# Batches and heads change places in an attention with routed experts: loads, stores, denominators and the order of the work

## The chip, the cores and the metric

One core of a Trainium2 chip runs the kernel. The metric is the device time of one execution in microseconds (us), the median of several runs.

## The reference

Two stages follow each other. First a linear attention over q, k, v of shape (8 batches, 8 heads, 576 tokens, 64), all float32:

```python
def phi(x):
    proj = np.einsum('bhsd,df->bhsf', x, w_phi)              # 64 -> 128 features
    proj = proj - np.max(np.abs(proj), axis=-1, keepdims=True)
    return np.concatenate([np.exp(proj), np.exp(-proj)], axis=-1)
q_p, k_p = (phi(q), phi(k))
kv = np.einsum('bhsf,bhsd->bhfd', k_p, v)
z = np.sum(k_p, axis=2)
num = np.einsum('bhsf,bhfd->bhsd', q_p, kv)
den = np.einsum('bhsf,bhf->bhs', q_p, z)[..., None] + 1e-06
attn = num / den
```

Its output is 4608 tokens of 512 values. Then 8 experts: `logits = x @ w_gate` are sorted over all tokens and experts at once, each token goes to the first expert in that order that still has room (576 tokens each), and each expert computes `relu(x @ w1) @ w2` with 512, 1024 and 512 columns.

## The kernel before, in words

**Units.** The attention goes by 16 units; a unit is a pair of batches and a pair of heads. Of the 128 rows of every tile, one half belongs to one member of a pair and the other half to the other. In a unit the steps are, by the names used below:

- SyncE issues the loads: ki and qi (`loadx`, L131, through `raw`, L116: 8 DMAs of 72 KB each, in pieces of 32 rows) and vi (`loadv`, L125: two DMAs of 64 rows). ki, qi and vi have two buffers each.
- VectorE transposes blocks (kt, qt, L183: kT and qT).
- TensorE projects k and q in three groups each (kg, qg, L194; 72 matmuls of 64x64, 24 a group), VectorE takes the largest magnitude (kgm, qgm, L198) and subtracts it (kgs, qgs, L201); for two of the k groups ScalarE copies (kgc, L207) and GpSimd subtracts (L210).
- ScalarE takes the exponentials of k (ke, L222: kP), TensorE multiplies with v (kv, L241, three groups of 24), GpSimd sums kP over the tokens (ad, L231 and L232: ks).
- ScalarE copies kv (kvT, L245), TensorE multiplies it with the gate weights beside an identity (bd, L257), ScalarE copies the result (kz, L260), TensorE sums ks over the rows (z, L272, the denominators, 32 matmuls of 64x64 against ones), VectorE puts that beside kz (zk, L274).
- TensorE transposes the q part (T, L288), ScalarE takes its exponentials (ex, L292: qP), TensorE multiplies (num, L305, 144 matmuls of 128x64, in two groups), and VectorE divides (x0 and x1, L309 to L320: xp). A store takes xp to memory (xs): ScalarE issues it for the first 13 units, SyncE for the last three (L325). GpSimd adds the logits (lg, L331 to L333).

A matmul on float32 stands as two instructions in the trace, so the counts here are of the trace's instructions.

**What sets the order.** Class `Plan` keeps a list of steps, each with an engine, a duration, a due time and what it waits for. In the attention `strict` is on: on each engine the steps stand in the order of their due times, 16 a unit apart plus an offset out of the table `ATT['o']` (`place`, L152; rows '0', '1', 's' for all units between, '9' for the last). Every engine's queue is in order, so a step that waits holds what stands behind it. In addition each k load from unit 4 on waits for the first exponentials of the unit two before it (L135 and `kel`). Seven matmuls on zeros (L111) keep TensorE busy before the first data.

**After the attention** comes the routing (a search by digits of the logits, small steps of VectorE and TensorE), and then the experts, whose order `Plan` works out from the due times in the table `MOE` and modelled durations. Their products are h (L885) and y (L915, L930).

Of the kernel before, what the change touches and what calls it, by code (L numbers as in the profile page):

```python
# [17 lines left out]
class Plan:  # L18
# [3 lines left out]
    SEM=40.; strict=False; dl=0.; wp=6.; fetch=0.; at=16.; edge=193.; ready=0.  # L22
# [5 lines left out]
    def order(self):  # L28
# [7 lines left out]
        while left:  # L36
# [61 lines left out]
def attention(ctx, tc, nc, q, k, v, w_phi, w_gate, xs, L, C, xp, cfg={}, after=None, later=None, count=None, init=iter(())):  # L98
# [3 lines left out]
    d=dict(TI=17.,ldk=60.,ldq=50.,ldv=45.,kt=-8.,kg=0.,ks=3.,kv=8.,kvs=1.,bd=1.,z=5.,qt=-4.,qg=4.,qs=3.,T=5.,num=20.,ns=4.,stay=3.,init=-6.,nqP=4,pools=(('kg',0),('kg',1)),nkt=3,nqt=3,ad=4.,st=5.,sem=85.,pr=6.,prs=2.5,fetch=3700.)  # L102
# [8 lines left out]
    for _ in range(cfg.get('nwarm',7)): PE.matmul(p[:,0],w[:,0:128],w,start=True,stop=True)  # L111
# [4 lines left out]
    def raw(eng,t,x,u,bi):  # L116

        bp,hp=divmod(u,NP)
        for a in range(2):
            for db in range(2):  # L120
                o=bass.AP(tensor=x.tensor,offset=x.offset+((2*bp+bi)*H+2*hp+a)*HS+32*db,ap=[[18*D,32],[D,18],[1,32]])
                i=eng.dma_start(t[64*a+32*db:64*a+32*db+32,bi],o)  # L122
                if a==db==0: first=i
        return first
# [6 lines left out]
    def loadx(nm,x,u):  # L131
        t=T[nm,u]=sb.tile([128,2,18,32],F32,name=nm+'i',bufs=2)
        for bi in range(2):
            i=raw(nc.sync,t,x,u,bi)
            if nm=='k' and u>3 and bi==(u>7): tc.add_manual_dep(i.ins,T['kel',u-2].ins.name,mybir.DependencyInfo(mybir.DependencyClass.Sync,mybir.DependencyReason.DATA),reason='behind the exponentials')  # L135

    T['k',0]=sb.tile([128,2,18,32],F32,name='ki',bufs=2); T['q',0]=sb.tile([128,2,18,32],F32,name='qi',bufs=2)
    raw(nc.sync,T['k',0],k,0,0); raw(nc.scalar,T['k',0],k,0,1)
    raw(nc.sync,T['q',0],q,0,0); raw(nc.scalar,T['q',0],q,0,1)
    P=Plan(d['stay']*1e3); P.SEM=d['sem']; P.fetch=d['fetch']  # L140
    P.add(('boot',-1),'SP',8900.,-1e3,lambda x: None)
    P.add(('aboot',-1),'ACT',10300.,-1e3,lambda x: None)
# [9 lines left out]
    def place(name,eng,u,due):  # L152

        t=d.get('o')
        if t is None: return due
        if name=='st' and eng=='ACT': return u*16.+66.7
        if eng=='X': return due
        if name=='ldv' and eng=='SP': return u*16.+t['1'].get('ldv.SP',t['s']['ldq.SP']+.01)
        return u*16.+t['s' if eng=='SP' else {0:'0',1:'1',NU-1:'9'}.get(u,'s')][(name if isinstance(name,str) else ''.join(map(str,name)))+'.'+eng]
    def unit(u):  # L160
# [8 lines left out]
        if not first:  # L169
            add('ldk','SP',6600.,-d['ldk'],lambda x: loadx('k',k,u),slot=slots(('ki',2)),lat=4000.)  # L170
            add('ldq','SP',6600.,-d['ldq'],lambda x: loadx('q',q,u),slot=slots(('qi',2)),lat=4000.)
            if u>1: add('ldv','SP',1300.,-d['ldv'],lambda x: loadv(u),slot=slots(('vi',2)),lat=5000.)
            else: add('ldv','X',0.,-d['ldv'],lambda x: loadv(u,G),slot=slots(('vi',2)),after=9000.)
        else:
            add('ldv','X',0.,-d['ldk'],lambda x: loadv(u,G),slot=slots(('vi',2)),after=9000.)
            for nm in 'kq': add('ld'+nm,'X',0.,-d['ldk'],lambda x: None,slot=slots((nm+'i',2)))

        def blocks(nm,aft):

            for bi in range(2):  # L180
                def f(x,bi=bi):
                    if bi==0: T[nm+'T',u]=sb.tile([128,2,9,32,2],F32,name=nm+'T',bufs=2)
                    V.transpose(T[nm+'T',u][:,bi].rearrange('p s t l -> p l s t'),T[nm,u][:,bi])  # L183
                add((nm+'t',bi),'DVE',662.,d[nm+'t']+.7*bi,f,['ld'+nm],slot=slots((nm+'T',2)) if bi==0 else (),frees=((nm+'i',u),),after=aft[u][bi] if u<len(aft) else 0.,seq=(nm+'t',0) if bi else None)
        def project(nm,g,s0,s1,due,src):
# [16 lines left out]
            add((nm,g),'PE',n*(218. if not first else 480. if nm=='kg' else 340.),due,pe,[(src[0]+'t',0),(src[0]+'t',1)],'Q',slots(('g',NG,nm,g)),((src,u),),ins=16*n+.5)  # L202
# [45 lines left out]
        def bd(x):  # L248
            p=T['bdp',u]=pair(('g',u,'bd'))(x)
            t=T['kvT',u]  # L250
            for i in range(2):
                for fh in range(2):
                    for a in range(2):
                        r=slice(64*a,64*a+64)
                        for c in range(2):
                            o=128*fh+64*c
                            PE.matmul(p[64*c:64*c+64,a,72*(2*i+fh):72*(2*i+fh)+72],t[r,i,o:o+64],C['bd'][r,hp,:],start=True,stop=True)  # L257
# [5 lines left out]
        def z(x):  # L263
            p=T['zp',u]=pair(('g',u,'z'))(x)
            ks=T['ks',u]
            for a in range(2):
                for fh in range(2):
                    for i in range(2):
                        r=slice(64*i,64*i+64)
                        for c in range(2):  # L270
                            o=128*fh+64*c
                            PE.matmul(p[64*c:64*c+64,i,2*(2*fh+a):2*(2*fh+a)+2],ks[r,a,o:o+64],C['one'][r,0:2],start=True,stop=True)  # L272
        def zk(x):
            V.tensor_copy(T['kz',u].rearrange('p i h a e -> p i (h a) e')[:,:,:,72],T['zp',u][:,:,0:8:2])  # L274
        add('z','PE',430.,kend+d['z'],z,[('ad',8)],'Q',slots(('g',NG,'z')),(('ks',u),),ins=65)
        add('zk','DVE',180.,kend+d['z']+.5,zk,['z','kz'],frees=(('g',u,'z'),))

        blocks('q',((12600.,12700.),))
        for g,(s0,s1) in enumerate(SG):
# [13 lines left out]
            add(('T',g),'PE',2*n*62.,due+d['T'],tr,[('qgs',g)],'P',slots(('g',NG,'T',g)),(('qgt',u,g),),ins=8*n+1)  # L293
# [71 lines left out]
def consts(ctx,tc,nc,w_phi):  # L365
# [7 lines left out]
    nc.vector.tensor_scalar(ident,jp,0.0,None,op0=OP.is_equal)  # L373
    one=cp.tile([128,128],F32,name='one'); nc.vector.memset(one,1.0); C['one']=one
    return C

def weights(ctx,tc,nc,w_gate,C):
    cp=ctx.enter_context(tc.tile_pool(name='wts',bufs=1))
    W=dict(C)
    bd=cp.tile([128,4,72],F32,name='bd'); W['bd']=bd  # L380
    g=w_gate.rearrange('(h a d) e -> a d h e',a=2,d=64)
    for i in range(2):
        r=slice(64*i,64*i+64)
        nc.vector.tensor_copy(bd[r,:,8-8*i:72-8*i],C['ident'][r,None,64*i:64*i+64].to_broadcast([64,4,64]))
        nc.gpsimd.dma_start(bd[r,:,64*i:64*i+8],g[i])
# [568 lines left out]
MOE = {'TE': 48.88, 'ch': -31.55, 'cp': 1.18, 'w1': 52.42, 'w2': 22.65, 'xt': 37.52, 'hl': -10.26, 'g': -10.06, 'y': 48.5, 'w20': 11.59, 'c1': -22.58, 'cp1': 0.52, 'stay': 7.96, 'sem': 96.08, 'wp': 124.82}  # L954
# [58 lines left out]
```

## Time and profile before

| | us |
|---|---|
| three runs | 776.07, 777.0, 781.02 (median 777.0) |
| the profiled execution | 778.89 |
| its span, first to last instruction | 777.1 |
| busy: PE | 735.8 (95%) |
| PEld (weight loads) | 640.2 (82%) |
| DVE (VectorE) | 563.0 (72%) |
| ACT (ScalarE) | 348.2 (45%) |
| POOL (GpSimd) | 310.0 (40%) |

PE is TensorE, SP is SyncE; SPq and ACTq are the queues in which they issue transfers. A row of a timeline has its start, its length, the engine, the line, what is written and read, and in brackets how long the engine stood idle before it and what ended that. The granted clock (PEclk) is a share of full speed.

### The profile page before, as it was taken

How to read it: one execution, taken by the hardware profiler on the slowest of the kernel's cores; microseconds unless marked ns; L12 is line 12 of the kernel's file. 1: busy time of each engine (PE TensorE's matmuls, PEld its weight loads, DVE VectorE, ACT ScalarE, POOL GpSimd, SP SyncE). 2: the span in 40 equal slices, each digit the busy share in tenths (PEclk: the TensorE clock that was granted, in tenths of full speed). 3: DMA queues.
4: the chain of work that ended last, by engine and by line, in shares of the span. 5: the costliest groups of instructions: out<-in, count | busy, mean ns of one | idle time of the engine just before them, and what ended most of it. 6: DMA issues, size and time to landing. Idle time of an engine off the chain costs nothing.

```text
span 777.1 us, 25979 instructions
## 1 busy us (share of the span) xinstructions
PE 735.8 (95%) x11090; PEld 640.2 (82%) x11090; DVE 563.0 (72%) x1489; ACT 348.2 (45%) x609; POOL 310.0 (40%) x331
## 2 busy tenths in 40 slices
PE   5988999899999995899999999999999999999997
PEld 3777888888888885598798898898897897897995
DVE  7985988788889867898597597696696795671410
ACT  2775776677766650343243333333332422352411
POOL 6877788688778750201302202203104104301102
PEclk9998999999999995899999999999999999999999
DMA  9677878777776211534505505505406407601301
GB/s 152 98 141 146 161 137 168 146 153 148 141 138 141 68 35 32 169 110 139 191 11 154 183 5 163 177 2 181 158 2 196 143 1 237 244 29 42 129 14 47
DMA packets 206403, 91.95 MB, mean 118 GB/s; under 512 B 154784, under 2 KB 189632, under 8 KB 206288
## 3 DMA queue, kind: packets, MB, share of 16 engines
q1 hardware_dynamic: 179952, 61.89, 33.8%
q0 software_dynamic: 6416, 20.15, 7.8%
q10 hardware_dynamic: 19920, 8.26, 3.9%
q8 instruction: 87, 1.43, 0.7%
q14 instruction: 28, 0.23, 0.1%
HBM read 71.39 MB, written 18.87 MB: 116 GB/s over the span
## 4 chain that ended last, share of the span: by engine, by line
PE 73%; issue 13%; DVE 4%; DMA 3%; ACT 2%; POOL 2%; SPq 2%; POOLq 0%; ACTq 0%; DVEq 0%
PE h L885 20%; PE y L915 17%; PE g L305 10%; PE g L241 7%; PE g L194 6%; PE y L930 3%; PE g L288 3%; SPq L122 2%; DMA qi<-in_q_dram 2%; DMA ki<-in_k_dram 2%; PE rps L619 1%; PE g L257 1%; PE rps L615 1%; PE h L853 1%; POOL out_dram L945 1%
## 5 line engine op out<-in xcount | busy, mean ns | idle before, releaser
L945 POOL DMA_INDIRECT out_dram<-ysb,idx x40 | 42.4, 1059 | 331.0 <-ACT ysb L938 328.4
L232 POOL TENSOR_TENSOR ks<-ks,kP 128x512 f32<-128x512 f32 x112 | 143.0, 1277 | 21.9 <-ACT kP L222 15.6
L885 PE MATMUL h<-xh,w1h 128*128 128x272 f32 (+3 forms) x512 | 141.6, 301 | 0.0
L885 PE MATMUL h<-xh,w1l 128*128 128x272 f32 (+3 forms) x512 | 140.5, 296 | 0.2 <-DVE w1l L826 0.2
L897 ACT ACTIVATE fh<-h 128x272 fp32r<-128x272 f32 (+2 forms) x128 | 49.2, 386 | 128.9 <-PE h L885 103.9
L915 PE MATMUL y<-w2h,fh 128*128 128x512 f32 x256 | 101.8, 398 | 0.0
L915 PE MATMUL y<-w2h,fl 128*128 128x512 f32 x256 | 100.8, 394 | 0.0
L915 PE MATMUL y<-w2l,fh 128*128 128x512 f32 x256 | 100.7, 394 | 0.0
L885 PEld LDWEIGHTS h<-xh,w1l 128*128 128x128 f32 x512 | 96.7, 189 | 0.4 <-DVE w1l L826 0.4
L885 PEld LDWEIGHTS h<-xh,w1h 128*128 128x128 f32 x512 | 96.1, 189 | 1.0 <-ACT xh L858 0.5
L885 PE MATMUL h<-xl,w1h 128*128 128x272 f32 (+3 forms) x512 | 92.6, 298 | 0.0
L305 PE MATMUL g<-kz,qP 128*64 128x73 f32 x2304 | 85.6, 235 | 5.8 <-issue 5.5
L305 PEld LDWEIGHTS g<-kz,qP 128*64 128x64 f32 x2304 | 81.4, 143 | 8.8 <-issue 7.4
L292 ACT ACTIVATE qP<-g 128x768 f32<-128x768 f32 x96 | 70.8, 811 | 19.3 <-PE g L288 16.8
L222 ACT ACTIVATE kP<-kgt 128x768 f32<-128x768 f32 x96 | 74.0, 837 | 10.9 <-DVE kgt L201 6.7
L901 DVE SCALAR_TENSOR_TENSOR fl<-h,fh 128x272 fp32r<-128x272 f32 (+2 forms) x128 | 52.8, 417 | 32.9 <-ACT fh L897 18.2
L938 ACT COPY ysb<-y 128x512 f32<-128x512 f32 (+1 forms) x40 | 21.8, 546 | 121.9 <-issue 79.6
L885 PEld LDWEIGHTS h<-xl,w1h 128*128 128x128 f32 x512 | 75.7, 188 | 0.1
L241 PE MATMUL g<-kP,vi 64*64 64x256 f32 x1152 | 73.8, 377 | 1.8 <-ACT kP L222 1.7
L860 DVE TENSOR_TENSOR xl<-h,xh 128x512 fp32r<-128x512 f32 (+1 forms) x40 | 24.3, 626 | 56.1 <-ACT xh L858 54.8
L241 PEld LDWEIGHTS g<-kP,vi 64*64 64x64 f32 x1152 | 46.5, 133 | 13.2 <-ACT kP L222 2.2
L915 PEld LDWEIGHTS y<-w2l,fh 128*128 128x128 f32 x256 | 48.2, 188 | 9.9 <-issue 0.2
(203 smaller groups left out, 1334.9 us busy)
## 6 DMA issues: line engine op xcount, KB each, us to landing
raww<-in_moe_w_dram SPq DMA_DIRECT2D x64, 512.0 KB
ki<-in_k_dram SPq DMA_DIRECT2D x124, 72.0 KB
qi<-in_q_dram SPq DMA_DIRECT2D x124, 72.0 KB
vi<-in_v_dram SPq DMA_DIRECT2D x28, 288.0 KB
xs<-xp ACTq DMA_DIRECT2D x13, 576.0 KB
xs<-xp SPq DMA_DIRECT2D x3, 576.0 KB
vi<-in_v_dram POOLq DMA_DIRECT2D x4, 288.0 KB
xg<-xs,idx POOLq DMA_INDIRECT x40
```

The source lines that it names most:

```text
L194: PE.matmul(p[64*bi:64*bi+64,a,128*(s-s0):128*(s-s0)+128],t[r,bi,s,:],C['w'][r,:],start=True,stop=True)
L222: for i in range(2): z=A.activation(o[:,:,:,128*i:128*i+128],t,AF.Exp,scale=1.0-2*i)
L232: else: G.tensor_add(ks,ks,kP[:,s])
L241: PE.matmul(p[64*a:64*a+64,i,0:256],v_[r,a,s,:],kP[r,s,a,:],start=s==0,stop=s==8,skip_group_check=True)
L292: for fh in range(2): A.activation(t[:,fh].rearrange('p i a s t -> p i (a s t)'),p,AF.Exp,scale=1.0-2*fh)
L305: PE.matmul(p[64*ab:64*ab+64,a,73*(j-j0):73*(j-j0)+73],T['qP',u,j//3][:,fh,ab,a,j%3,:],T['kz',u][:,ab,fh,a,:],start=fh==0,stop=fh==1)
L860: p,h,l=T['xv',r,b0,i]; V.tensor_sub(l,p,h)
L885: PE.matmul(p,ws[:,k,o:o+128],xx[:,k,o1:o2],start=n==0,stop=n==11)
L897: A.activation(hh[:,f,o1:o1+m1],p[:,0:m1],AF.Relu)
L901: V.scalar_tensor_tensor(hl[:,f,o1:o1+m1],p[:,0:m1],0.0,hh[:,f,o1:o1+m1],op0=OP.max,op1=OP.subtract)
L915: PE.matmul(p,hx[:,f,o:o+128],ws[:,f%2,:],start=n==0,stop=n==23)
L945: st=G.indirect_dma_start(out=ov,out_offset=bass.IndirectOffsetOnAxis(ap=iv,axis=0),in_=yv,in_offset=None)
```

## The change

Of a unit's four batch and head combinations, the row halves now hold the two heads of one batch and the free dimension the two batches; before it was the other way round. Two heads lie next to each other in memory, so v comes with one DMA of 128 rows. The denominators take both row halves at once, against a matrix `sel` with ones in one half per column, 16 instructions of 128x64 in place of 32 of 64x64. All stores are issued by SyncE. The waits of k loads for exponentials are gone. 33 warm-up matmuls stand in place of 7; kt and qt tiles have 4 buffers in place of 3, qP 5 in place of 4. The tables of due times are new, with rows of their own for units 2 ('2') and 14 ('8') too, and the `MOE` table has new values.

```diff
-    for _ in range(cfg.get('nwarm',7)): PE.matmul(p[:,0],w[:,0:128],w,start=True,stop=True)
+    for _ in range(cfg.get('nwarm',33)): PE.matmul(p[:,0],w[:,0:128],w,start=True,stop=True)
...
-                o=bass.AP(tensor=x.tensor,offset=x.offset+((2*bp+bi)*H+2*hp+a)*HS+32*db,ap=[[18*D,32],[D,18],[1,32]])
+                o=bass.AP(tensor=x.tensor,offset=x.offset+((2*bp+a)*H+2*hp+i)*HS+32*db,ap=[[18*D,32],[D,18],[1,32]])
...
-        for i in range(2):
-            o=bass.AP(tensor=v.tensor,offset=v.offset+((2*bp+i)*H+2*hp)*HS,ap=[[9*D,64],[HS,2],[1,9*D]])
-            eng.dma_start(t[64*i:64*i+64].rearrange('p h s d -> p h (s d)'),o)
+        o=bass.AP(tensor=v.tensor,offset=v.offset+(2*bp*H+2*hp)*HS,ap=[[9*D,128],[H*HS,2],[1,9*D]])
+        eng.dma_start(t.rearrange('p h s d -> p h (s d)'),o)
...
-            if nm=='k' and u>3 and bi==(u>7): tc.add_manual_dep(i.ins,T['kel',u-2].ins.name,mybir.DependencyInfo(mybir.DependencyClass.Sync,mybir.DependencyReason.DATA),reason='behind the exponentials')
...
-                    for i in range(2):
-                        r=slice(64*i,64*i+64)
-                        for c in range(2):
-                            o=128*fh+64*c
-                            PE.matmul(p[64*c:64*c+64,i,2*(2*fh+a):2*(2*fh+a)+2],ks[r,a,o:o+64],C['one'][r,0:2],start=True,stop=True)
+                    for c in range(2):
+                        o=128*fh+64*c; e=2*(2*fh+a)
+                        PE.matmul(p[64*c:64*c+64,0,e:e+2],ks[:,a,o:o+64],C['sel'],start=True,stop=True)
...
-                                PE.matmul(p[64*ab:64*ab+64,a,73*(j-j0):73*(j-j0)+73],T['qP',u,j//3][:,fh,ab,a,j%3,:],T['kz',u][:,ab,fh,a,:],start=fh==0,stop=fh==1)
+                                PE.matmul(p[64*ab:64*ab+64,a,73*(j-j0):73*(j-j0)+73],T['qP',u,j//3][:,fh,a,ab,j%3,:],T['kz',u][:,a,fh,ab,:],start=fh==0,stop=fh==1)
...
-            (A if out_ else nc.sync).dma_start(o,T['x',u][:,:,8:136])
-        out_=u<13
-        add('st','ACT' if out_ else 'SP',700.,d['num']+d['ns']+d['st'],st,[('x',1)],lat=3500.,frees=(('xb',u),))
+            nc.sync.dma_start(o,T['x',u][:,:,8:136])
+        add('st','SP',d['sp'],d['num']+d['ns']+d['st'],st,[('x',1)],lat=3500.,frees=(('xb',u),))
...
-    for u in range(4,NU): P.by[('ldk',u)]['deps'].append((('ke',0),u-2))
```

What the new due times say, sorted by engine, for a unit u in the steady part:

| engine | before | after |
|---|---|---|
| SyncE | k(u), v(u-1), q(u) | st(u-4), q(u), v(u-1), k(u) |
| TensorE | kg0, kg1, kv0(u-1), kg2, qg2, kv1(u-1), qg0, kv2(u-1), qg1, bd(u-1), z(u-1), T2, T0, num0(u-1), num1(u-1), T1 | kg0, kv0(u-1), kg1, kg2, kv1(u-1), qg0, kv2(u-1), qg2, bd(u-1), qg1, z(u-1), T0, T2, num0(u-1), num1(u-1), T1 |
| ScalarE | the store of u-2 behind the first exponentials of u | no store |

On VectorE, x1(u-2) stands just ahead of the maxima of kg0(u), with the second q transpose of unit u right behind those. In SyncE's new order the k load of unit 14 stands between those of units 7 and 8, and VectorE's two transposes of it stand in units 7 and 9.

## Rows read from the trace of the kernel before

**Rows 1.** Busy time in stretches: length, engines busy (instructions), PEclk, DMA share, GB/s

```profile
60.00:80.00 20.00, 16.92 (x436) 15.58 (x432) 12.11 (x19) 10.74 (x15) 13.02 (x11) 0.83 0.80 161
440.13:497.13 57.00, 57.00 (x456) 49.39 (x457) 43.42 (x148) 19.91 (x43) 10.70 (x15) 1.00 0.36 117
```

**Rows 2.** Timeline of TensorE, undisturbed units and the last one: start, length

```profile
78.33 1.54 PE L194 MATMUL g<-w,kT 64*64 64x128 f32 x48
...
88.45 4.79 PE L305 MATMUL g<-kz,qP 128*64 128x73 f32 x144
...
93.69 1.54 PE L194 MATMUL g<-w,kT 64*64 64x128 f32 x48
...
261.38 1.54 PE L194 MATMUL g<-w,kT 64*64 64x128 f32 x48
...
283.65 6.40 PE L305 MATMUL g<-kz,qP 128*64 128x73 f32 x144
```

**Rows 3.** Timeline of TensorE, 56 to 78 us

```profile
56.17 0.89 PE L194 MATMUL g<-w,kT 64*64 64x128 f32 x24 [1.45 <-ACT qP L292]
...
68.05 0.77 PE L257 MATMUL g<-bd,kvT 64*64 64x72 f32 x32 [3.08 <-ACT kvT L245]
...
70.98 6.90 PE L305 MATMUL g<-kz,qP 128*64 128x73 f32 x144
```

**Rows 4.** Timeline of ScalarE and its queue, 51 to 68 us

```profile
51.05 0.58 ACTq L325 DMA_DIRECT2D xs<-xp  x1
51.68 3.05 ACT L222 ACTIVATE kP<-kgt 128x768 f32<-128x768 f32 x4 [2.65 <-DMA qi<-in_q_dram]
...
66.81 0.56 ACTq L325 DMA_DIRECT2D xs<-xp  x1
67.41 0.58 ACT L245 COPY kvT<-g 128x512 f32<-128x512 f32 x1 [4.28 <-DMA qi<-in_q_dram]
```

**Rows 5.** Busy time in stretches around one stop of TensorE

```profile
134.00:137.00 3.00, 2.97 (x108) 2.63 (x106) 2.97 (x6) 2.15 (x5) 2.04 (x2) 1.00 1.03 256
137.00:140.00 3.00, 1.00 (x30) 1.00 (x32) 1.22 (x2) 2.91 (x5) 2.65 (x3) 1.00 0.61 93
140.00:143.00 3.00, 3.00 (x60) 3.00 (x58) 0.84 (x3) 1.51 (x2) 2.84 (x3) 0.55 0.93 205
```

**Rows 6.** Waits: total us, times, longest (TensorE 78-262, SyncE 60-250, VectorE 0-300)

```profile
PE g L305 <- issue: 5.3, 6, 2.0
PE g L288 <- issue: 0.9, 1, 0.9
...
SPq L122 <- ACT kP L222: 10.6, 8, 2.6
...
DVE rd L309 <- PE g L305: 30.4, 26, 3.8
```

**Rows 7.** Queues of the page: packets, MB, share of 16 DMA engines

```profile
q8 instruction: 87, 1.43, 0.7%
```

**Rows 8.** Timeline of SyncE's queue, one unit's loads

```profile
180.15 7.31 SPq L122 DMA_DIRECT2D ki<-in_k_dram  x8
187.56 2.19 SPq L130 DMA_DIRECT2D vi<-in_v_dram  x2
189.86 6.57 SPq L122 DMA_DIRECT2D qi<-in_q_dram  x8
```

**Rows 9.** Timeline of TensorE, bd and the denominators of one unit

```profile
86.43 0.73 PE L257 MATMUL g<-bd,kvT 64*64 64x72 f32 x32
86.98 0.59 PE L272 MATMUL g<-one,ks 64*64 64x2 f32 x32
```

**Rows 10.** Timeline of TensorE, warm-up, first projection, later matmuls on zeros

```profile
1.36 3.17 PE L111 MATMUL g<-warm 128*128 128x512 bf16 x7 [1.36 <-DVE warm L109]
10.22 4.32 PE L194 MATMUL g<-w,kT 64*64 64x128 f32 x72 [5.70 <-DVE kT L183]
...
319.88 1.03 PE L582 MATMUL y<-onesb 128*128 128x512 bf16 x4
```

More of the change, by code (lines that the diff above doesn't have):

```diff
@@ L18 @@
 class Plan:
-    SEM=40.; strict=False; dl=0.; wp=6.; fetch=0.; at=16.; edge=193.; ready=0.
+    SEM=40.; strict=False; dl=0.; wp=6.; fetch=0.; at=16.; edge=193.; ready=0.; sw=(45.,45.)
     def __init__(self,stay=0.): self.t=[]; self.by={}; self.stay=stay
@@ L77, in order @@
             if e=='PE':
-                if mode[0] not in (None,x['mode']): s+=95.
-                if mode[0]!=x['mode'] or s>free.get(e,0.)+1.: s+=100. if x['mode']=='A' else 50.
+                if mode[0] not in (None,x['mode']): s+=45.
+                if mode[0]!=x['mode'] or s>free.get(e,0.)+1.: s+=self.sw[x['mode']!='A']
                 mode[0]=x['mode']
@@ L183, in f @@
                     V.transpose(T[nm+'T',u][:,bi].rearrange('p s t l -> p l s t'),T[nm,u][:,bi])
-                add((nm+'t',bi),'DVE',662.,d[nm+'t']+.7*bi,f,['ld'+nm],slot=slots((nm+'T',2)) if bi==0 else (),frees=((nm+'i',u),),after=aft[u][bi] if u<len(aft) else 0.,seq=(nm+'t',0) if bi else None)
+                add((nm+'t',bi),'DVE',662.,d[nm+'t']+.7*bi,f,['ld'+nm],slot=slots((nm+'T',2)) if bi==0 else (),frees=((nm+'i',u),),after=aft if first else 0.,seq=(nm+'t',0) if bi else None)
         def project(nm,g,s0,s1,due,src):
@@ L201, in sub @@
                 V.tensor_sub(t,vw(),T[nm+'m',u,g].to_broadcast([128,2,n,128]))
-            add((nm,g),'PE',n*(218. if not first else 480. if nm=='kg' else 340.),due,pe,[(src[0]+'t',0),(src[0]+'t',1)],'Q',slots(('g',NG,nm,g)),((src,u),),ins=16*n+.5)
+            add((nm,g),'PE',n*(218. if not first else d['cold'][nm]),due,pe,[(src[0]+'t',0),(src[0]+'t',1)],'Q',slots(('g',NG,nm,g)),((src,u),),ins=16*n+.5)
             add((nm+'m',g),'DVE',dv(256*n),due+.8,mx,[(nm,g)])
@@ L256, in bd @@
                             o=128*fh+64*c
-                            PE.matmul(p[64*c:64*c+64,a,72*(2*i+fh):72*(2*i+fh)+72],t[r,i,o:o+64],C['bd'][r,hp,:],start=True,stop=True)
+                            PE.matmul(p[64*c:64*c+64,a,72*(2*i+fh):72*(2*i+fh)+72],t[r,i,o:o+64],C['bd'][r,272*hp+72*i:272*hp+72*i+72],start=True,stop=True)
         def kz(x):
@@ L354, in some @@
                 if i<NI-1: break
-        P.add(('init',i),'DVE',270. if i<7 else 200.,-100.+i if i<7 else 457.+.001*i,some,[('init',i-1)] if i else [],lat=95.,after=3900.)
+        early=i<d['ni']
+        P.add(('init',i),'DVE',300. if early else 200.,(-100.+i if d.get('o') is None else d['o']['i']['init%d'%i]) if early else 457.+.001*i,some,[('init',i-1)] if i else [],lat=95.,after=d['iaft'])
+        if not early: P.t[-1]['key']=('F','late')
+    P.by[(('pr',0),NU-NP-1)]['deps'].append(('init',d['ni']-1))
     P.strict='o' in d
-    for u in range(4,NU): P.by[('ldk',u)]['deps'].append((('ke',0),u-2))
     out=P.order()
@@ L373, in consts @@
     nc.vector.tensor_scalar(ident,jp,0.0,None,op0=OP.is_equal)
+    sel=cp.tile([128,2],F32,name='sel'); C['sel']=sel
+    nc.vector.memset(sel,0.0)
+    for i in range(2): nc.vector.memset(sel[64*i:64*i+64,i:i+1],1.0)
     one=cp.tile([128,128],F32,name='one'); nc.vector.memset(one,1.0); C['one']=one
@@ L379, in weights @@
     W=dict(C)
[L380 to L385, printed above, removed]
+    bd=cp.tile([128,4*272],F32,name='bd'); W['bd']=bd
+    g=w_gate.rearrange('(h d) e -> d h e',d=64)
+    for a in range(2):
+        r=slice(64*a,64*a+64)
+        nc.vector.tensor_copy(bd.rearrange('p (h z) -> p h z',z=272)[r,:,8:136].rearrange('p h (i e) -> p h i e',e=64),C['ident'][r,None,None,64*a:64*a+64].to_broadcast([64,4,2,64]))
+        nc.gpsimd.dma_start(bd.rearrange('p (h z) -> p h z',z=136)[r,:,0:8],g)
     return W
```

50 lines of the change are left out of this document (20 added, 30 removed).

## The prediction

> **What bounds the kernel now.** I read the busy time in stretches first [rows 1]. From the experts' first product on, TensorE is busy for all of the time at clock 1.00: an expert's period, 57.00 us, is 57.00 us busy. The reader is to see that no order can shorten that part much, for nothing else is waited for. The routing between the two halves, a chain of small steps, the change doesn't touch. What is open to gain is the attention, up to 290 us (283.65 + 6.40 [rows 2]). Its TensorE timeline [rows 2] shows what a unit costs: the first k projection of unit 4 starts at 78.33, that of unit 5 at 93.69, so one undisturbed unit is 15.36 us; that of unit 15 starts at 261.38. Eleven units took 183.05 us, 16.64 each, against 169.0 at the undisturbed rate: 14.1 us are lost in this stretch, and more before it.
>
> Where they are lost, the waits say. Early, TensorE stands still 1.45 us for the exponentials of ScalarE, then 3.08 us for its copy kvT [rows 3]. ScalarE's own timeline [rows 4] names the cause: both times it stood idle, 2.65 and 4.28 us, until a transfer of q had landed, and the instruction that was released then is the issue of the store of xp on ScalarE's queue (51.05 and 66.81). So a store at the head of ScalarE's queue held back the activations behind it. The stretch 60 to 80 has clock 0.83 [rows 1]: after the 3.08 us stop, the output product (num, 144 matmuls) took 6.90 us [rows 3] against 4.79 undisturbed [rows 2]. Later, from 78 to 262, almost all of TensorE's idle time is put down to "issue" (5.3 + 0.9 = 6.2 us [rows 6]): nothing in the program is waited for. At 136 the DMA engines are at 1.03 and 256 GB/s, the next 3 us have PE at 1.00 us busy, and the 3 us after that run at clock 0.55 [rows 5]. The instruction queue moves 1.43 MB in 87 packets [rows 7], 16 KB each; I read these stops as TensorE's instructions coming late while a store and loads crowd the DMA engines.
>
> **The change part by part.**
>
> *Stores from ScalarE to SyncE.* ScalarE no longer holds a store, so the waits of 1.45 + 3.08 us go, and with the stop its slow num, 6.90 - 4.79 = 2.11 us. Sum 6.64 us. What is late next is VectorE, but between 60 and 80 it is busy 12.11 of 20 us [rows 1], so it has 7.9 us to give there. I take -6.6, bounds -6.6 (all) and 0 (if the loads are late in any case: the store waited for a q load, and that load is still as late).
>
> *What the store costs on SyncE.* SyncE issues per unit 8 k, 2 v and 8 q transfers: 7.31 + 2.19 + 6.57 = 16.07 us [rows 8], of the 16.64 that a unit takes. It is as full as TensorE. The v load in one transfer takes one issue away and the store adds one: 18 before, 18 after, so the count is level; by one issue of either sort at the mean of a k load (7.31/8 = 0.91) the balance is 0, with ends -0.9 and +0.9 a unit if the two differ by a whole one. In the new order a store of unit n stands ahead of the q load of unit n+4, its v and its k. It waits for VectorE's x1 of n; the q load behind it waits anyway for a buffer that VectorE's transpose of q(n+2) frees, and that transpose follows x1(n) on VectorE by a few instructions. So the new wait is mostly covered by one that was there. If the cover is gone, the 17 load issues behind the store start late, and units wait for k and q. I take +1 us in all, bounds 0 and the price of the rival below.
>
> *The waits of k loads for the exponentials removed.* They cost SyncE 10.6 us in 8 waits between 60 and 250 [rows 6], none of which reached TensorE by itself; I take 0, and keep what this gives as room for the store.
>
> *The stops of the instruction fetch.* Of the 14.1 us lost between 78 and 262, the 6.2 us idle and what follows at half clock hang on bursts where a store on ScalarE's queue runs beside loads on SyncE's. With both on one queue they follow each other. The denominators need 16 instruction pairs a unit in place of 32, so each unit has 888 TensorE instructions in place of 920. Bounds: 0 (bursts stay) and -14.1 (all goes). Only the longest of the six stops of num, 2.0 us [rows 6], has its DMA burst among my rows, and with its slow stretch (3 us at 0.55, so 1.4 us lost) it is worth 3.4; I take -4, near to that.
>
> *Denominators in column halves.* Before, 32 matmuls of 64x64 in 0.59 us [rows 9], 18 ns each. After, 16 of 128x64, the form of num: 4.79/144 = 33 ns [rows 2], so 0.53 us: -0.06 a unit, -1 us in 16, bounds -1 and +1 (two switches of form more around it; bd in front of it keeps 0.73 for 32 [rows 9]). I take 0. A rule speaks against a gain here: by the Trainium skill (TensorE: Matmul & The Clock Gate, section "The mechanism") a weight load runs under a running matmul only where the two use different rows of the array; weights on all 128 rows can't. The 33 ns of num against 18 ns agree with it, and by the rule alone the halved count would be worth nothing.
>
> *The swap itself* leaves every projection, kv, bd, transpose and num at its count and shape: 0.
>
> *33 warm-up matmuls in place of 7.* The 7 take 3.17 us, 0.45 each, and the first 72 projection matmuls 4.32 us, 60 ns each [rows 10], against 1.54/48 = 32 ns later [rows 2]. Kept busy until the k block lands at 10.2, the engine should start at the higher level: of the first third (24 matmuls) 24 x 28 ns = 0.7 us are on the path, the rest lies under VectorE. Bounds: 33 at the late rate 1.03/4 = 0.26 [rows 10] end at 1.36 + 8.5 = 9.9; all at 0.45 they end at 16.2 and delay the first projection by 6.0. I take -0.7.
>
> *More buffers (kt and qt 4, qP 5), new due times, new order of the experts.* The undisturbed unit is already dense in TensorE work, the experts too [rows 1]: 0, bounds -3 and +3. One place looks tight: unit 14's k load is put between those of units 7 and 8 and holds one of the two ki buffers for two units; with an issue of 7.31 us [rows 8] and a landing behind it, it just fits into a unit of 16.64. 0 to +4 (as long as ScalarE's longest wait for a q transfer, 4.28 [rows 4]); I take 0.
>
> **Sum.** -6.6 + 1 - 4 - 0.7 = -10.3 us. The profiled execution took 778.9 (span 777.1 and 1.8 around it), so 768.6 on its basis; it lies 0.2% above the median of 777.0, on which the sum gives 766.7. I put 767.0.
>
> **Rivals.**
>
> *B. Only the stores' block goes.* The bursts stay, for bytes and packets are the same, and the fetch stops with them. For it: the DMA share is 0.80 already in 60 to 80 with both queues [rows 1]. Against it: the worst stop follows the one stretch at 1.03. -6.6 - 0.7 + 1 = -6.3, and 1 to 4 us back from the tight place: 777.0 - 6.3 + 2.5 = 773.2. By the Trainium skill (DMA: Bandwidth & Descriptors, section "Issuing engines are not separate DMA queues") transfers from all engines share the same DMA engines and interleave, and another issuing engine saves only issue time; that is this rival, and the 0.80 agrees.
>
> *C. The new order reaches the undisturbed rate.* All 14.1 us of the steady part go, and 1 or 2 at the experts' edges: 777.0 - 6.6 - 0.7 - 14.1 - 1 = 754.6. Against it: SyncE's 16.07 us a unit [rows 8] is above 15.36 [rows 2].
>
> *D. Slower: SyncE becomes the bound.* The store waits at the head of the queue for x1 with 17 load issues behind it. It decides from the point where the issues and the wait exceed the unit TensorE has now: 16.07 [rows 8] + w > 16.64, w over 0.6 us that no load's own wait covers. VectorE waits up to 3.8 us for num ahead of x [rows 6]; with w = 2.5 a unit is 18.6, 2.0 us more in 12 units, +24, less 6.6 + 0.7: 793.7. For it: the queue has no room. Against it: the load behind the store waits for VectorE at nearly the same place, and a load has a buffer's lead of most of a unit.
>
> **How the numbers follow.** Forecast (761 to 772) 0.48, B 0.29, C 0.12, D 0.11. A measurement of this kernel tells about 1% from no change, 7.8 us here: faster is under 769.2, slower above 784.8. Faster takes C and nearly all of the forecast's: 0.58; same has B and the forecast's rest: 0.33; slower most of D: 0.09. The range leaves out half of C's low side and most of D: 754 to 782.
>
> **What would show it.** ScalarE without a wait for q transfers between 46 and 70; no TensorE stop at kvT and no clock under 0.95 in 60 to 80; units at 16.0 to 16.3 us from unit 4 on; num of unit 15 ending near 280 in place of 290; the experts at 57.0 as before. Wrong would be: TensorE waiting for VectorE's kT or qT behind k or q transfers (D, or the tight place around units 8 and 9); a first projection after 11 us; an expert over 57.5.

## The result, and the profile after

The change made the kernel about 1% slower; the prediction was 767.0, 10 us faster.

| | before | after |
|---|---|---|
| median of 15 runs each (lowest to highest) | 777.15 (773.28 to 781.46) | 784.79 (781.13 to 788.9) |
| ratio, with its 95% interval | | 1.0099 [1.0077, 1.0121] |
| profiled execution, its span | 778.89, 777.1 | 784.79, 782.7 |

All of the loss lies in the attention. Timeline of TensorE of the kernel after (start, length, what; in brackets the idle time before and what ended it):

```profile
36.79 0.40 PE L183 MATMUL g<-w,kT 64*64 64x128 f32 x2 [2.14 <-DVE kT L172]
...
38.84 3.63 PE L291 MATMUL g<-kz,qP 128*64 128x73 f32 x80
...
78.34 0.89 PE L183 MATMUL g<-w,kT 64*64 64x128 f32 x24
...
110.05 0.89 PE L183 MATMUL g<-w,kT 64*64 64x128 f32 x24
...
129.44 1.93 PE L183 MATMUL g<-w,kT 64*64 64x128 f32 x21 [3.25 <-DVE xp L306]
...
146.85 0.89 PE L183 MATMUL g<-w,kT 64*64 64x128 f32 x24
...
204.77 4.80 PE L291 MATMUL g<-kz,qP 128*64 128x73 f32 x144
...
210.02 0.89 PE L183 MATMUL g<-w,kT 64*64 64x128 f32 x24
...
228.05 0.40 PE L183 MATMUL g<-w,kT 64*64 64x128 f32 x2 [2.38 <-DVE xp L306]
229.50 1.34 PE L183 MATMUL g<-w,kT 64*64 64x128 f32 x19 [1.04 <-DVE kT L172]
...
242.83 4.80 PE L291 MATMUL g<-kz,qP 128*64 128x73 f32 x144
...
249.43 1.49 PE L183 MATMUL g<-w,kT 64*64 64x128 f32 x48
...
288.69 6.97 PE L291 MATMUL g<-kz,qP 128*64 128x73 f32 x144
```

The last num ends at 288.69 + 6.97 = 295.66, in the kernel before at 290.05 [rows 2]: 5.6 us later, and the spans differ by 5.6. What follows takes 487.0 us in both. The reader is to see three things. Unit 4 starts at 78.34, before at 78.33: what was gained up to there has been used up, at the start. From unit 8 (146.85) to unit 12 (210.02) a unit takes 15.79 us, in place of 16.64. And two stretches of two units are far longer than 31.6: units 6 and 7, 110.05 to 146.85, 36.80; units 12 and 13, 210.02 to 249.43, 39.41. These two stops lose 5.2 + 7.8 = 13.0 us. (Taken from num to num, 204.77 to 242.83, the second loses 6.5; the rest is that unit 14's first k projections stand later in the order than those of other units.) At the start, num of unit 0 begins at 38.84; in the kernel before (its timeline of TensorE) it began 7.35 us sooner:

```profile
31.49 5.48 PE L305 MATMUL g<-kz,qP 128*64 128x73 f32 x144
```

What was foreseen for the middle is there. Busy time in stretches of the kernel after; the first answers to [rows 1], the next hold the stops, the last is an expert's period:

```profile
60.00:80.00 20.00, 19.82 (x552) 17.46 (x548) 17.98 (x30) 13.77 (x20) 14.36 (x11) 1.00 0.73 135
120.00:140.00 20.00, 16.71 (x430) 14.42 (x428) 13.48 (x22) 10.83 (x16) 13.60 (x12) 0.91 0.77 160
220.00:240.00 20.00, 16.53 (x374) 14.14 (x374) 12.38 (x19) 9.81 (x14) 13.77 (x13) 0.83 0.83 180
440.00:497.00 57.00, 57.00 (x456) 49.19 (x455) 43.95 (x148) 19.79 (x42) 10.08 (x15) 1.00 0.36 113
```

TensorE's waits of the kernel after between 78 and 262 us (total, times, longest) answer to [rows 6]:

```profile
PE g L183 <- DVE xp L306: 5.6, 2, 3.2
PE g L291 <- issue: 1.1, 2, 0.6
PE g L183 <- DVE kT L172: 1.0, 1, 1.0
```

The stops of "issue" fell from 6.2 us to 1.1. New are the waits for VectorE's xp. Why VectorE is late, its timeline says, and below it that of SyncE's queue:

```profile
128.38 0.91 DVE L306 TENSOR_TENSOR xp<-g,rd 128x720 f32<-128x720 f32 x1 [4.28 <-DMA xs<-xp]
...
225.82 0.78 DVE L172 STREAM_TRANSPOSE kT<-ki 128x576 f32<-128x576 f32 x1 [4.30 <-DMA ki<-in_k_dram]
```

```profile
107.36 14.00 SPq L122 DMA_DIRECT2D ki<-in_k_dram  x16
121.45 1.38 SPq L311 DMA_DIRECT2D xs<-xp  x2
...
195.52 15.14 SPq L122 DMA_DIRECT2D ki<-in_k_dram  x16
210.76 0.64 SPq L311 DMA_DIRECT2D xs<-xp  x1
211.50 6.79 SPq L122 DMA_DIRECT2D qi<-in_q_dram  x8
218.39 0.57 SPq L127 DMA_DIRECT2D vi<-in_v_dram  x1
219.06 7.33 SPq L122 DMA_DIRECT2D ki<-in_k_dram  x8
```

At 107 SyncE issues 16 k transfers in a row, those of unit 7 and of unit 14, and two stores stand behind them. Sorted by the new due times, SyncE's order there is: store of unit 3, q of 7, v of 6, k of 7, k of 14, store of 4, store of 2, q of 8; the trace has the same sequence. So the two stores are those of units 4 and 2. Unit 2's was given a place behind unit 4's, though VectorE had written its values by 79.13. Until they land near 128 both xp buffers are held, and VectorE can't divide for unit 5. Besides the k load of unit 14, the new due times thus move two more things of which the section on the change says nothing: unit 2's store, and the k load of unit 15. At 195 SyncE issues the k loads of units 12 and 15; unit 13's keys come only at 219, and VectorE waits for them until 225.82.

### The profile page after: what moved, and what is told of

Read it like the earlier page. It is cut to its first block, busy times and chain, and to the rows that moved or that the text cites. A ratio compares the mean times of both kernels' runs of the same rounds, so it can differ in the third digit from the quotient of the medians.

```text
span 782.7 us, 25440 instructions
## 1 busy us (share of the span) xinstructions
PE 746.7 (95%) x10860; PEld 638.8 (82%) x10860; DVE 571.0 (73%) x1492; ACT 346.2 (44%) x609; POOL 307.1 (39%) x329
## 4 chain that ended last, share of the span: by engine, by line
PE 74%; issue 7%; DVE 7%; SPq 6%; DMA 3%; ACT 1%; POOL 1%; POOLq 0%; DVEq 0%
PE h L875 23%; PE y L905 20%; PE g L291 7%; PE g L229 6%; SPq L122 6%; PE g L183 6%; PE y L920 3%; PE g L274 2%; PE rps L609 1%; PE h L843 1%; PE rps L605 1%; PE g L245 1%; DMA qi<-in_q_dram 1%; PE g L258 1%; DMA xs<-xp 1%
## 5 line engine op out<-in xcount | busy, mean ns | idle before, releaser
L935 POOL DMA_INDIRECT out_dram<-ysb,idx x40 | 39.6, 990 | 336.1 <-ACT ysb L928 324.5
L875 PE MATMUL h<-xh,w1l 128*128 128x304 f32 (+3 forms) x512 | 142.1, 297 | 0.0
L875 PE MATMUL h<-xh,w1h 128*128 128x272 f32 (+3 forms) x512 | 139.7, 301 | 0.8 <-ACT xh L848 0.4
L291 PE MATMUL g<-kz,qP 128*64 128x73 f32 x2304 | 81.1, 232 | 1.1 <-issue 1.1
L291 PEld LDWEIGHTS g<-kz,qP 128*64 128x64 f32 x2304 | 78.1, 140 | 3.2 <-issue 2.0
L199 POOL TENSOR_TENSOR kgt<-kgt,kgm 128x768 f32<-128x768 f32 x30 | 44.1, 1469 | 34.3 <-ACT kgt L196 34.3
L229 PEld LDWEIGHTS g<-kP,vi 64*64 64x64 f32 x1152 | 44.7, 137 | 14.1 <-issue 1.3
```

The costliest lines, as they stand in the source:

```text
L199: G.tensor_sub(t,t,T[nm+'m',u,g].to_broadcast([128,2,n,128]))
L229: PE.matmul(p[64*a:64*a+64,i,0:256],v_[r,a,s,:],kP[r,s,a,:],start=s==0,stop=s==8,skip_group_check=True)
L875: PE.matmul(p,ws[:,k,o:o+128],xx[:,k,o1:o2],start=n==0,stop=n==11)
```

## Experiments

In all of them the unit of comparison is the kernel before on the same chip (medians 773.6 to 774.9), so 0.001 of a ratio is 0.77 us.

### The k loads that stand too early

Only due times change (row '8' is unit 14, row '9' unit 15, row '2' unit 2):

```diff
-'8': 'ldk.SP': -155.893, 'kt0.DVE': -84.31, 'kt1.DVE': -53.021
+'8': 'ldk.SP': -44.629, 'kt0.DVE': 12.447, 'kt1.DVE': 15.136
-'2': 'st.SP': 44.578
+'2': 'st.SP': 16.0
-'9': 'ldk.SP': -92.373
+'9': 'ldk.SP': -58.4
```

> The kernel after, with three due times put back in turn: the k load and k transposes of unit 14, the k load of unit 15 and the store of unit 2 stand where those of a steady unit stand. Theory A (the k loads put far ahead of their use hold SyncE's full queue for some 7 us each, and what stands behind them comes late): both long stops go, units 6 to 8 take 31 to 32 us in place of 36.8 and units 12 to 14 about 32 in place of 39.4, so 11 us less: 772 to 776. Rival B (the stores at the head of SyncE's queue are the cause, whatever the k loads do): stops of the same length come again at some stores, 781 to 786.

The last line alone:

> The kernel after with the k load of unit 15 alone put back in turn. Theory A: the stop of VectorE for k of unit 13 (4.30 us, near 221) goes and with it the slow clock behind it, 5 to 7 us less, 778 to 780; the stop near 124 stays. Rival B: as the kernel after, 783 to 787.

Measured: all three lines 1.0035 [1.0000, 1.0070], the last line alone 1.0047 [1.0022, 1.0072], the change itself 1.0099. In the profile of the first neither stop is left; TensorE's timeline, units 4 and 11 and the last num:

```profile
77.56 0.89 PE L183 MATMUL g<-w,kT 64*64 64x128 f32 x24
...
187.51 0.89 PE L183 MATMUL g<-w,kT 64*64 64x128 f32 x24
...
277.79 7.09 PE L291 MATMUL g<-kz,qP 128*64 128x73 f32 x144
```

Seven units take 109.95 us, 15.71 each, and the last num ends at 284.88, 10.8 us before that of the change. This profile is of one of the fastest executions (773.81, median 778.16); by the ratios the three lines bring 0.0064, 5 us, where theory A asked for 11. Of the stores, that of unit 2 now goes out next to unit 1's (SyncE's queue):

```profile
79.92 1.39 SPq L311 DMA_DIRECT2D xs<-xp  x2
```

In the profile of the second the later stop is gone and the first one stays:

```profile
130.59 1.93 PE L183 MATMUL g<-w,kT 64*64 64x128 f32 x21 [5.24 <-DVE xp L306]
```

So unit 15's early load costs 0.0052, 4 us (5 to 7 were expected), and the later stop is shown to come from where it stands. With the other two lines the profile gains the first stop too, but the medians only another 0.0012, inside the intervals. These two lines, unit 14's load and unit 2's store, were not tried apart. By SyncE's order the first stop needs both: with unit 14's load in turn the two stores would go out some 7 us sooner, and VectorE waited 4.28; with unit 2's store in turn a buffer would have been free long before. This is an argument from the order, not shown by a run. Mended, the new order is still no faster than before.

### The stores' queue

ScalarE again issues the stores, in the new order:

```diff
-            nc.sync.dma_start(o,T['x',u][:,:,8:136])
+            (A if u<13 else nc.sync).dma_start(o,T['x',u][:,:,8:136])
```

> The kernel after with the stores of units 0 to 12 issued by ScalarE again, each ahead of the first copy of k two units later. Theory A: SyncE gets 0.6 us a unit back, the stop near 124 (VectorE waits for a store) shrinks, the one near 221 stays: 2 to 4 us less, if nothing comes back. Theory E (two queues at once are what made TensorE's instructions late): TensorE's idle time put down to issue in the product num rises from 1.1 us towards the 5.5 of before, 3 to 5 us more, which eats that gain. Rival B: the whole loss against before goes, 776 to 779.

Measured 1.0190 [1.0149, 1.0231]: 0.0091, 7 us, slower than the change. TensorE's idle time behind "issue" stayed near 1 us, so in this order the store's queue doesn't make those stops.

The cleaner pair keeps every edit and takes the due times of before, so that TensorE's groups stand in the order of before; the two differ in the stores' queue alone:

> The changed code, every edit of it kept (swap, one transfer for the values, denominators in 16 matmuls, stores on SyncE, 33 warm-ups), but laid out by the due times of the kernel before, so that TensorE runs the matmul groups in the order of before. Theory A (the edits are worth some 5 us, and the new due times lose more than that: at the start, where after is 211 matmuls behind before at 40 us, and at the two places where a k load stands too early on SyncE): 767 to 772 where before has 774, ratio 0.990 to 0.998; num of unit 0 begins near 31.5 to 33.5 us (38.84 in after, 31.49 in before), no idle time above 2 us behind VectorE's xp. Theory F (an edit itself costs the start its time: the swapped loads, the longer warm-up): as after or between, ratio 1.003 to 1.010, num of unit 0 at 36 us or later.

> The kernel of the label e7_old_order with the stores of units 0 to 12 issued by ScalarE at the due times of before, so that the two differ in the stores' queue alone. If the prediction's sum for the stores holds (waits of 1.45 and 3.08 us and the slow num, 6.6 us in all), this is 4 to 7 us slower than e7_old_order, and ScalarE waits again for q transfers between 46 and 70 us. If SyncE's stores give that back elsewhere, the two are within 2 us.

Measured 1.0002 [0.9977, 1.0027] with SyncE's stores and 1.0101 [1.0055, 1.0146] with ScalarE's: 0.0099, 7.7 us for the queue. (For the first, both theories had put the ratio and the start of num elsewhere: it lies between them.) In the second, ScalarE's timeline has the wait of [rows 4] again, in one piece, and TensorE stands behind it:

```profile
63.48 0.59 ACTq L312 DMA_DIRECT2D xs<-xp  x1
64.12 3.04 ACT L212 ACTIVATE kP<-kgt 128x768 f32<-128x768 f32 x4 [11.53 <-DMA qi<-in_q_dram]
```

```profile
68.61 1.56 PE L184 MATMUL g<-w,kT 64*64 64x128 f32 x24 [10.59 <-ACT qP L279]
```

The prediction's largest term is thus borne out. It is the price of the queue with all other edits in place, where ScalarE waits once for 11.53 us; the kernel before with nothing but its stores moved was not run. Read the other way, all edits but the stores' queue, in the old order, cost 0.0101, 7.8 us (TensorE's stop behind the store is 10.59 us there, 1.45 + 3.08 in the kernel before); so with the gain of the stores they only reach the time of before. The profile of e7_old_order, with the old order and the stores on SyncE, shows two places where it was given back, here TensorE's timeline at the start and near 245 us, and VectorE's at the latter:

```profile
35.37 4.80 PE L291 MATMUL g<-kz,qP 128*64 128x73 f32 x144
...
245.12 2.84 PE L229 MATMUL g<-kP,vi 64*64 64x256 f32 x24 [4.23 <-issue]
```

```profile
243.16 0.78 DVE L172 STREAM_TRANSPOSE kT<-ki 128x576 f32<-128x576 f32 x1 [4.82 <-DMA ki<-in_k_dram]
```

Num of unit 0 begins 3.9 us after that of before, in the same order of work. And a late k load stops TensorE near 242 us: 4.23 us here, 5.53 (e14_old_order_late_gate) and 6.87 (e19_values_in_two) in others with this order, none in e11_old_order_warm7 and e10_old_order_stores_scalar. The profile puts these stops down to "issue"; I put them down to the load, because VectorE waits for keys just before each, 4.82, 6.13 and 7.54 us, always 0.6 to 0.7 longer than TensorE.

### The start

First, unit 0's loads dealt out between the two queues by batch, as before, not by head:

> The kernel after; of unit 0's loads SyncE issues those of one batch and ScalarE those of the other, as before the change, where after it they share by head. Theory C (the two queues read places close together in memory, and each packet of 128 bytes takes 18 to 19 ns in the first 12 us in place of 14): packets back at 14 ns, the first k transpose at 9.4 to 9.6 us in place of 10.54, the total 1 to 2 us less. Rival D (the warm-up, the larger gate load or the swap itself slows them): first transpose stays at 10.5, total within 1 us.

Measured 1.0077 [1.0051, 1.0104], num of unit 0 at 38.88: no gain, and the packets of 128 bytes stayed at 18 to 19 ns on the mean of the first 12 us (before: 14), so theory C falls. (At about 18 us TensorE then waited 3.31 us for qT.) Then the number of warm-ups, in three kernels:

> The kernel before with 33 warm-up matmuls in place of 7, nothing else. Theory W (the warm-ups, which in the changed kernel run beside unit 0's loads until 11 us, slow those loads): the 128-byte packets of the first 12 us take 18 to 20 ns instead of 14, the first projection begins 1 us later, num of unit 0 at 34 to 35.5 us instead of 31.49, and the time rises by 2 to 4 us, ratio 1.002 to 1.006. Theory C (the swapped addresses and the larger gate load make the packets slow, not the warm-ups): packets stay at 14 ns, the first projection takes 2.2 us instead of 4.3, num of unit 0 by 31.5 us, ratio 0.997 to 1.001.

> The kernel of the label e7_old_order with 7 warm-up matmuls in place of 33. Theory W: packets of the first 12 us at 14 to 15 ns, num of unit 0 near 32 us instead of 35.37, time 3 us under that of e7_old_order, so a ratio of 0.995 to 0.998 and the first version faster than before. Theory C: packets stay at 18 ns or more, the first projection runs at half speed and is 2 us longer, num of unit 0 at 36 us or later, ratio 1.000 to 1.004.

> The kernel of the label e1_k_loads_in_turn (the changed kernel with its early k loads and store put in turn) with 7 warm-up matmuls in place of 33. Theory W: first kT by 9.6 us instead of 10.5, num of unit 0 near 35 us instead of 37.45, ratio 0.998 to 1.001 against 1.0035. Theory C: start no earlier, first projection 2 us longer, ratio 1.003 to 1.006.

Measured 0.9981 [0.9954, 1.0009], 1.0007 [0.9978, 1.0035] and 1.0037 [1.0008, 1.0067], none to be told from the kernel it was made from. Packets: 13.6 ns with 33 warm-ups before, 19.9 with 7 in the old order, 21.5 in the mended new one (means over SyncE's queue in the first 12 us, worked out from the trace's packet records, as in the expectations). Theory W falls. Timeline of TensorE, the kernel before with 33 warm-ups:

```profile
1.36 10.26 PE L111 MATMUL g<-warm 128*128 128x512 bf16 x33 [1.36 <-DVE warm L109]
11.67 2.20 PE L194 MATMUL g<-w,kT 64*64 64x128 f32 x72
...
31.90 4.79 PE L305 MATMUL g<-kz,qP 128*64 128x73 f32 x144
```

The first projection starts 1.5 us later than in [rows 10], right behind the last warm-up, but takes 2.20 instead of 4.32, and num of unit 0 begins at 31.90 instead of 31.49.

Third, the load of the gate's weights, which the swap doubled:

```diff
-        nc.gpsimd.dma_start(bd.rearrange('p (h z) -> p h z',z=136)[r,:,0:8],g)
+        gl.append((bd.rearrange('p (h z) -> p h z',z=136)[r,:,0:8],g))
...
+        if u==1:
+            for x in C['gl']: nc.gpsimd.dma_start(*x)
```

> The kernel of the label e7_old_order with the load of the gate's weights (two transfers, 16 KB each, in elements of 32 bytes) issued behind the values of unit 1 instead of ahead of them. Theory G (between 4 and 9 us this load makes every 128-byte packet of unit 0's k and q take 20 to 28 ns instead of 13; the swap doubled it, since each row half now needs the weights of all heads, and that is what the start lost): packets of the first 12 us at 13 to 15 ns, both kT done by 11 us, first q projection near 17 us instead of 19.1, num of unit 0 at 31.5 to 33 us instead of 35.37, time 2.5 to 4 us below e7_old_order, ratio 0.995 to 0.997. Theory S (the swapped order of addresses or of partitions makes them slow): packets stay near 20 ns, num of unit 0 near 35 us, ratio 1.000 as for e7_old_order.

> The kernel of the label e1_k_loads_in_turn with the same late load of the gate's weights. Theory G: first kT by 9.6 us, num of unit 0 1 to 3 us before its 37.45 (in this order unit 2's keys stand before it and may hold it), ratio 0.997 to 1.002 against 1.0035. Theory S: start and ratio as there, 1.002 to 1.006.

Measured 1.0010 [0.9983, 1.0038] and 1.0010 [0.9981, 1.0039]; num of unit 0 at 34.94 and 38.33. Between 5 and 9 us the packets still took 21 to 24 ns on the mean. Theory G falls for the most part: the gate load isn't needed for the slow packets. Part of it holds: VectorE's first transpose of keys began at 9.32 and 9.49, in place of 10.28 (e7_old_order) and 10.15 (e1_k_loads_in_turn), and the second ratio lies where G put it. In the first of the two the 33 warm-ups then held the first projection until 11.41; the late load with 7 warm-ups was not tried.

Last, an order pieced together: units 0 to 2 by the due times of before, the rest by the mended new ones, and the same with unit 0's loads by batch:

> The loads of units 14 and 15 and the store of unit 2 in turn, as in the first experiment, and besides units 0 to 2 by the due times of the kernel before on all engines but SyncE, so that TensorE's order at the start is that of before (first kv before the queries' projections, unit 2's keys behind unit 0's num). Theory A: num of unit 0 begins by 33 us instead of 37.45, and what that brings stays: ratio 0.990 to 0.998, against 1.0035 of the first experiment. Theory F: num of unit 0 begins early or late, but the time stays at 1.002 or above, because what the start gains is waited out behind the loads of units 2 to 4.

> The kernel of the label e8_turn_old_start with unit 0's k and q loads dealt out to SyncE and ScalarE by batch, as in before, instead of by head. Both theories: no more than 1 us either way against e8_turn_old_start (the same split alone moved the changed kernel by 781.19/781.6, nothing that can be told); the 128-byte packets of the first 12 us stay near 18 ns.

Both missed: 1.0277 [1.0229, 1.0326] and 1.0302 [1.0243, 1.0361]. Where the two orders meet, ScalarE's copies come late (TensorE's longest wait for kgt is 6.05 and 8.06 us), so these runs tell nothing about the start.

### Issues or transfers on SyncE

SyncE issues loads almost without a gap from 10 to 245 us. If its issues set the pace, fewer of them would help. Two column halves in one transfer:

```diff
-            for db in range(2):
-                o=bass.AP(tensor=x.tensor,offset=x.offset+((2*bp+a)*H+2*hp+i)*HS+32*db,ap=[[18*D,32],[D,18],[1,32]])
-                eng.dma_start(t[64*a+32*db:64*a+32*db+32,i],o)
+            o=bass.AP(tensor=x.tensor,offset=x.offset+((2*bp+a)*H+2*hp+i)*HS,ap=[[32,2],[18*D,32],[D,18],[1,32]])
+            eng.dma_start(t[64*a:64*a+64,i],o)
```

> The kernel of the label e7_old_order with each load of keys or queries issued as 4 transfers of 64 partitions (144 KB) instead of 8 of 32 (72 KB), in the same pieces of 128 bytes. Theory Q (with the stores on it, SyncE issues loads without a gap from 10 to 245 us, so its issues, some 0.88 us each, set the pace): the issues take 0.9 to 1.1 us each, SyncE has gaps of 4 us or more a unit, late k loads (4.82 us of VectorE at 243 us) go, ratio 0.985 to 0.993. Theory T (the transfers themselves, in 128-byte pieces, set the pace, and an issue only waits its turn behind them): an issue takes 1.6 us or more, no gaps, ratio 0.998 to 1.003.

> The kernel of the label e1_k_loads_in_turn with the same 4 transfers a load. Theory Q: ratio 0.985 to 0.993 against 1.0035, units at 15.3 to 15.6 us, the end of the attention by 283 us in most executions. Theory T: 1.001 to 1.005.

> The changed kernel as it is, its order untouched, with 4 transfers a load instead of 8. Theory Q: the two stops near 124 and 221 us shrink (the 16 k transfers ahead of the store of unit 2 and ahead of unit 13's loads become 8, some 7 us earlier on SyncE), ratio 0.990 to 0.997 against 1.0099. Theory T: the stops stay as they are, ratio 1.007 to 1.012.

Measured 1.6659, 1.6733 and 1.6742 (1290 to 1296 us): neither theory. In the first, SyncE's queue (start, length) and busy time in a stretch:

```profile
110.61 21.64 SPq L121 DMA_DIRECT2D qi<-in_q_dram  x4
132.35 21.68 SPq L121 DMA_DIRECT2D ki<-in_k_dram  x4
154.15 5.26 SPq L126 DMA_DIRECT2D vi<-in_v_dram  x1
```

```profile
111.00:154.00 43.00, 18.11 (x354) 15.51 (x354) 11.31 (x16) 11.02 (x16) 8.10 (x8) 0.65 0.18 28
```

An issue takes 5.4 us and the DMA engines move 28 GB/s, against 161 in [rows 1]. By the trace's packet records no more than 4 packets of k and q are under way at once on SyncE's queue, in the kernel after up to 29; the value loads of the same slow kernel, still one transfer of 128 rows, reach 20. The Trainium skill has the rule (DMA: Bandwidth & Descriptors, section "Why a DMA increments its semaphore by 16 and not by 1"): a transfer is spread over the largest number of engines, up to 16, that divides the slowest dimension of both sides. Here that dimension is the 2 column halves, so 2 engines; the 4 packets agree with it, if an engine has two under way, as the 29 on 16 engines suggest. No run split the load in another way, so the rule is agreed with, not tested. Also to be seen: the one v issue behind them took 5.26 us, not 0.57. The length of an issue includes its turn behind the transfers ahead of it.

So the count was changed in another way, without touching k and q:

> The kernel of the label e7_old_order with the values of each unit loaded by two transfers (one a batch) instead of one: 14 issues more on SyncE, the same bytes in the same pieces. Theory Q (SyncE's issues, without a gap from 10 to 245 us, set the pace): each of the 14 costs its 0.57 us, the last q load is issued some 8 us later, ratio 1.007 to 1.011 against 1.0002 of e7_old_order. Theory T (the transfers set the pace): nothing is added, ratio 0.998 to 1.003.

> The kernel of the label e7_old_order with the values of units 2 to 15 issued by GpSimd (some 0.75 us each there, as for units 0 and 1) instead of SyncE: 14 issues fewer on SyncE. Theory Q: the last q load is issued 5 to 8 us earlier, ratio 0.990 to 0.996, and that is faster than before. Theory T: 0.998 to 1.003, or slower by what GpSimd's additions then lose.

Measured 1.0027 [0.9994, 1.0060] and 1.1736 [1.1691, 1.1780]. Fourteen more issues cost 0.0025, 2 us, where theory Q asked for some 8, and the 2 lie within the intervals; the last q load was issued at 247.9, in e7_old_order at 250.9. The issue count doesn't set the pace. The last kernel says nothing of it: I put the value load on GpSimd ahead of additions that the next kv needs, and it waits there for its buffer, 13 times:

```profile
99.11 0.74 POOL L127 DMA_DIRECT2D vi<-in_v_dram  x1 [13.78 <-PE g L230]
```

No version is shown to beat before. Nearest is before with 33 warm-ups, 0.9981, whose interval holds 1.

## Why the prediction was wrong, point by point

Two steps failed. The new due times were put at 0, and the runs give them 7.5 us. And the sum kept to its end what the stores gain, with the start of the changed kernel put at -0.7; there num of unit 0 came 7.35 us later.

- **Stores, -6.6: the mechanism held, and the size came near.** 7.7 us in the pair that differs in this alone (TensorE's stop 10.59 us in one piece), 7 in the new order (there ScalarE's long waits were 5.8 us for a k transfer and 4.6 for VectorE). ScalarE of the kernel after has no wait for a q transfer between 46 and 70 us (below, all its waits there), and 60 to 80 is at clock 1.00.

```profile
ACT kgt L196 <- DVE kgm L187: 2.9, 2, 2.1
ACT qP L278 <- PE g L274: 1.6, 2, 1.3
ACT kvT L233 <- PE g L229: 1.0, 2, 0.6
ACT kz L248 <- PE g L245: 0.8, 1, 0.8
```

- **Fetch stops, -4: wrong in cause; that the size came near is luck.** "With both on one queue they follow each other" was the reason given. Among TensorE's waits between 20 and 285 us those put down to "issue" sum to 7.0 before; with the edits in the old order and the stop near 242 left out 3.0 to 6.6 in five profiles, the one with ScalarE's stores having the 3.0; in seven profiles of the new order 0.9 to 3.4. So the queue of the stores is not their cause; the new order has the fewest, and what in it takes them away was not tried.
- **Store's cost on SyncE, +1: not measured by itself.** It is inside the 7.7 us of the pair. Fourteen more issues of value loads cost about 2 us, within the intervals.
- **Denominators and experts, 0: right.** The 16 matmuls take 0.63 us, the 32 took 0.59 [rows 9]; an expert takes 57.00. So the halved count was worth nothing, as foreseen. The prediction's comparison of 33 with 18 ns set matmuls of 73 columns beside those of 2; with 2 columns on both sides the 128x64 matmul takes 39 ns (0.63/16). The swap, the removed waits of k loads and the added buffers were not undone by themselves, so their 0 is not tested; they are among the edits that together cost 7.8 us in the old order.
- **Warm-ups, -0.7: not told from 0.** The first projection did come after 11 us, at 11.42: the 33 ended at 11.22, later than the 9.9 of the lower bound, and the first keys were transposed at 11.32. So the late keys alone would have held it nearly as long; with 33 warm-ups in the kernel before, and in the first kernel with the late gate load, where the keys are earlier, the warm-ups alone held it (11.67 and 11.41).
- **"The undisturbed unit is already dense in TensorE work": this step failed.** "More buffers, new due times, new order" was taken at 0 with bounds -3 and +3. The change (1.0099) and its edits in the old order (1.0002) lie 0.0097, 7.5 us, apart. Unit 15's load, which the prediction didn't see, is 4 us of it; the other 3.5 us are not taken apart.
- **"One place looks tight ... 0 to +4 ... I take 0": mis-sized.** The place was right, the wait was not: foreseen was TensorE waiting for keys behind a held ki buffer; in the trace VectorE waited 4.28 us for a store, and TensorE for VectorE's xp. In the profile this stop cost 5.2 us, above the bound, which was taken from ScalarE's wait for one transfer and not from the two stores queued behind the loads, one of them unit 2's, placed late; in the medians mending both brought 0.0012, 0.9 us, not told from 0.
- **The sum itself: what is gained early must last.** The sum kept the -6.6 to the end. Num of unit 0 began 7.35 us later, and by unit 4 the two kernels were level. With the old order it is 3.9 later, and there unit 0's q is late (below). With the new order q is hardly late (VectorE transposes it from 14.98, in place of 14.31), but unit 2's keys stand ahead of unit 0's num and TensorE waits 2.14 us for them. The prediction looked at the first projection only.

In the one profile the losses are 7.35 us at the start and 13.0 in the stops. As unit 4 starts level and the ends differ by 5.6, some 7.3 were gained up to unit 4 and 7.4 in the faster units; both are differences, not readings. Rival D named SyncE but not the mechanism: it was not a store waiting for x1, but loads placed ahead of stores and of other loads, and a store placed late. The range ended at 782; after was 784.79.

Why unit 0's loads land later in the changed kernel is settled in part. It is not the warm-ups, not the gate load alone, not the split by head or batch. For q in the old order the profiles point to the value loads of units 0 and 1: GpSimd issues them sooner there (6.79 us with 7 warm-ups, 9.50 before), beside unit 0's q. VectorE's first transpose of q, before and in the old order with 7 warm-ups:

```profile
14.31 0.77 DVE L183 STREAM_TRANSPOSE qT<-qi 128x576 f32<-128x576 f32 x1
...
17.84 0.78 DVE L172 STREAM_TRANSPOSE qT<-qi 128x576 f32<-128x576 f32 x1 [2.93 <-DMA ki<-in_k_dram]
```

In all seven profiles with the split by head and values issued at 6.1 to 6.8 us, this transpose begins at 17.7 to 18.5; in all six with values at 10.8 to 11.8, the change among them, at 13.9 to 15.1. No run moved the value loads of these two units alone, so it is a likely cause, not a shown one. What remains open is the slow packets from 5 to 9 us.

## What to carry to other kernels

Where each engine's queue is in order, a searched order is judged by what stands behind each early step: a load put ahead of its turn held a store, the store its buffer, and the buffer VectorE; another held the next unit's keys. Follow a gain through to a later mark (here the start of unit 4) before it goes into the sum. When transfers are merged, look at the slowest dimension first.

## What the runs showed that was not expected

- Merging two transfers of 72 KB into one of 144 KB, same pieces, took the kernel from 774 to 1290 us; the likely reason is its slowest dimension, which was 2.
- Pieces of 128 bytes took 13 ns each up to 4 us and, in the changed kernel, 20 to 28 from 5 to 9 us (15 to 19 from 5 to 7 us before); the cause is open.
- The same store issued by ScalarE held its activations for 11.53 us at one place, and with other due times 2.65 and 4.28 at two [rows 4]: such a wait is no constant. That it hangs on which loads are on their way is my reading.
